# Attention results re-laid with 128-column one-hot products, eight per unit instead of sixteen

## The chip, the cores and the metric

The kernel runs on one core of a Trainium2 chip. The metric is the device time of one execution in microseconds (us), as the median of several runs. Inputs and outputs are in the chip's main memory; the kernel loads them by DMA, computes on five engines that run side by side (PE for matrix products, DVE, ACT and POOL for elementwise work, SP for issuing transfers) and writes the result back.

## The reference

One decode step of a transformer layer: attention over a sliding window of a cache and a dense layer with the mish activation, both on the normalized input, added to the input.

```python
def reference(A_x, A_k_cache, A_v_cache, A_wq, A_wo, B_x, B_w1, B_b1, B_w2):
    # B=2, Sq=1, D=448; 16 query heads, 8 key heads, Dh=256, window W=4096 of 32768
    def _A_ref(x, k_cache, v_cache, wq, wo):
        q = (x @ wq).reshape(B, Sq, Hq, Dh).transpose(0, 2, 1, 3)
        k = jnp.repeat(k_cache[:, :, Sk - W:, :], rep, axis=1)
        v = jnp.repeat(v_cache[:, :, Sk - W:, :], rep, axis=1)
        p = _softmax(jnp.einsum("bhqd,bhkd->bhqk", q, k) * (Dh ** -0.5), axis=-1)
        o = jnp.einsum("bhqk,bhkd->bhqd", p, v)
        return o.transpose(0, 2, 1, 3).reshape(B, Sq, Hq * Dh) @ wo

    def _B_ref(x, w1, b1, w2):
        h = jnp.einsum("bsd,df->bsf", x, w1) + b1
        sp = jnp.log1p(jnp.exp(-jnp.abs(h))) + jnp.where(h > 0, h, 0)
        return jnp.einsum("bsf,fd->bsd", h * jnp.tanh(sp), w2)

    xn = _layernorm(A_x, axis=-1)
    return A_x + _A_ref(xn, A_k_cache, A_v_cache, A_wq, A_wo) + _B_ref(xn, B_w1, B_b1, B_w2)
```

Everything is bf16. The window of keys and values, 2 x 8 x 4096 x 256 numbers each, is by far the largest part of what is read.

## The kernel before

**Units.** The 8 key heads are taken in U = 4 units. A unit holds KU = 2 key heads for both batch rows, J = 4 pairs in all, and as rep = 2 query heads share a key head, NQ = 8 rows of scores. For each unit two k tiles of 4 MB (`load_k`, L97) and four v tiles of 2 MB (`load_v`, L105) are read, and the unit's rows of wo (`load_wo`, L112 and, for the last unit, L118). All of these are issued on SP's queue in the order of the program text; a load waits there until its buffer is free: two buffers for k, three for v (shared at the start with wq and w1), two for wo.

**Work of a unit.** DVE transposes the k tiles (`turns`, L269). PE computes scores (L336 for the mask, L347), ACT takes the exponential (L355), DVE transposes the result into the probabilities p (L358). `weigh` (L370, L378) sums them for the denominator. `values` (L392) multiplies p with the v tiles into PSUM, `gather` (L406 on ACT, L412 on PE) collects this into 8 columns per half, and `finish` (L439, DVE) divides by the denominator. What results is the tile `oT`: 128 partitions by (c, head, batch), where element m of partition p and c is result 2p + c of the head.

**Re-laying.** For units 0, 1 and 2, wo is read with 8 consecutive rows per partition, so that a partition of wo covers one key head and one query head and 8 neighbouring results. `relay` (L455, L464) brings oT into that order with one-hot matrices `hot` (set up on POOL at L147 and L149): for each of the two query heads h of a key head, four y and two k, a product of a 64-column one-hot matrix with the 4 columns of that head fills 64 rows of the PSUM tile `ox_ps`. ACT copies the whole to `ox` in bf16, and `mix_early` (L474) multiplies the 8 slices of ox with wo and adds to the accumulator `early`. The last unit has no relay: its wo is read in another order and `mix` uses oT directly (L249).

**Order.** The order of instructions on each engine is that of the program text. Relays of units 0 and 1 stand after `weigh(u + 1)`; PE goes on to the next unit's values after the mix. The relay of unit 2 stands in the last unit, after `values(3, 0)`; then come its mix, `carry` (L236, L238: the sum so far moves into the accumulator `acc`) and `values(3, 1)`.

**Start and end.** At the start the constants are set up on POOL and DVE, x is normalized, and `project` makes q from wq: its result is copied by ACT to `q_sb` (L300), transposed and spread into `qd`. The dense layer's first half runs early (L504 and on); its second half, `dense_out`, comes last. It multiplies the activation with w2, which arrives in four parts (L547) of 784, 448, 224 and 112 KB after the last v tile; 14 slices with four products each (L249), the last part holding one slice. Then DVE and ACT copy the four quarters of acc to `res` (L620, L622), and SP writes it out (L623).

Of the kernel before, what the change touches and what calls it, by code (L numbers as in the profile page):

```python
# [11 lines left out]
BF16 = mybir.dt.bfloat16  # L12
FP32 = mybir.dt.float32
# [4 lines left out]
def kernel(  # L18
# [13 lines left out]
    nc = tc.nc  # L32
    P = 128
# [5 lines left out]
    Bsz, Sq, D = A_x.shape  # L39
# [3 lines left out]
    rep = Hq // Hkv  # L43
# [3 lines left out]
    KU = J // Bsz  # L47
# [27 lines left out]
    consts = ctx.enter_context(tc.tile_pool(name="consts", bufs=1))  # L75
    small = ctx.enter_context(tc.tile_pool(name="small", bufs=2))
# [6 lines left out]
    ps_m = ctx.enter_context(tc.tile_pool(name="ps_m", bufs=1, space=PSUM))  # L83
# [54 lines left out]
    ident = consts.tile([P, P], BF16)  # L138
# [4 lines left out]
    nc.gpsimd.memset(ones[:], 1.0)  # L143
    id2 = consts.tile([Bsz, Bsz], FP32)
    nc.vector.tensor_copy(out=id2[:], in_=ident[0:Bsz, 0:Bsz])
    hot = consts.tile([P, KU, 4, 32, KU], BF16)
    nc.gpsimd.memset(hot[:], 0.0)  # L147
    for k in range(KU):
        nc.gpsimd.tensor_copy(  # L149
            out=hot[:, k, :, :, k], in_=ident[:].rearrange("p (q y) -> p y q", y=4)  # L150
        )
    eps_t = consts.tile([Bsz, 1], FP32)
    nc.vector.memset(eps_t[:], 1e-5)
# [7 lines left out]
        out=rstd[:], in_=mv[:, 1:2], func=ACT.Sqrt, bias=eps_t[:], scale=1.0  # L161
# [4 lines left out]
        out=xn_bf[:],  # L166
# [8 lines left out]
        out=parm[:], in_=ident[:].rearrange("p (a o) -> p o a", o=2), axis=AXIS.X, op=ALU.add  # L175
# [3 lines left out]
        out=jm[:],  # L179
        in_=ident[:].rearrange("p (a j h) -> p j a h", j=J, h=rep),  # L180
# [4 lines left out]
        out=jm[:], in0=jm[:], scalar1=-1.0, scalar2=29952.0, op0=ALU.add, op1=ALU.mult  # L185
# [3 lines left out]
        out=mneg[:], in_=jm[:].unsqueeze(1).to_broadcast([P, TH * 8, J])  # L189
    )  # L190
    sel = consts.tile([P, 2, NQ], FP32)
    for x in range(2):
        for w in range(4):
# [4 lines left out]
            else:  # L198
                nc.vector.tensor_tensor(
                    out=sel[:, x, :], in0=sel[:, x, :], in1=src, op=ALU.add  # L200
# [16 lines left out]
    for odd in range(2):  # L217
        for half in range(2):
            o = (half + odd) % 2
            nc.vector.tensor_scalar(  # L220
                out=xs[:, odd::2, half * Bsz : (half + 1) * Bsz],
# [55 lines left out]
    for n in range(2):  # L277
        for e in range(2):
# [3 lines left out]
                out=sp[:],  # L282
                in_=ident[:, o : o + 63 : 2].unsqueeze(1).to_broadcast([P, G, 32]),
# [3 lines left out]
    def project():  # L287
        q_ps = ps_m.tile([P, 512], FP32, tag="m", name="q_ps")
        for s in range(NS):
            for u in range(U):  # L290
                nc.tensor.matmul(  # L291
                    q_ps[32 * u : 32 * (u + 1), :],
                    lhsT=xs[:, s, :],
                    rhs=wq_t[s][:, u * 512 : (u + 1) * 512],
                    start=(s == 0),
                    stop=(s == NS - 1),
                    skip_group_check=True,
                )
        q_sb = consts.tile([P, 4, P], BF16)
        nc.scalar.copy(out=q_sb[:].rearrange("p a m -> p (a m)"), in_=q_ps[:])  # L300
        qt_ps = ps_m.tile([P, 4, P], BF16, tag="m", name="qt_ps")
        for a in range(4):
            nc.tensor.transpose(qt_ps[:, a, :], q_sb[:, a, :], ident[:])
        qT = consts.tile([P, 2, U, Bsz, KU, rep], BF16)
        q_v = qt_ps[:].rearrange("p (h c) (u r) -> p c u r h", c=2, u=U)
        for c in range(2):
            for b in range(Bsz):
                nc.vector.tensor_copy(
                    out=qT[:, c, :, b, :, :], in_=q_v[:, c, :, b : KU * Bsz : Bsz, :]
                )  # L310
        qr_ps = ps_m.tile([P, 2 * NB, U, NQ], FP32, tag="m", name="qr_ps")
        for n in range(NB):
            for e in range(2):
                nc.tensor.matmul(
                    qr_ps[:, 2 * n + e, :, :].rearrange("p u q -> p (u q)"),
                    lhsT=spread[n % 2, e][:].rearrange("p g a -> p (g a)"),
                    rhs=qT[:, n // 2].rearrange("p u b k h -> p (u b k h)"),
                    start=True,
                    stop=True,
                    skip_group_check=True,  # L320
                )
        for g in range(G):
            rows = slice(g * 32, (g + 1) * 32)
            nc.vector.tensor_copy(
                out=qd[rows, :, :, g, :],
                in_=qr_ps[rows].rearrange("p n u q -> p u n q"),
            )
# [119 lines left out]

    def relay(u):
        oT = state.pop(("oT", u))
        ox_ps = ps_m.tile([P, 4, 2, Bsz], FP32, tag="m", name="ox_ps")  # L450
        for h in range(rep):
            rows = slice(h * 64, (h + 1) * 64)
            for y in range(4):
                for k in range(KU):
                    nc.tensor.matmul(  # L455
                        ox_ps[rows, y, :, :],
                        lhsT=hot[:, k, y, :, :].rearrange("p q k -> p (q k)"),
                        rhs=oT[:, :, k * rep + h, :],
                        start=(y == 0 and k == 0),
                        stop=(y == 3 and k == KU - 1),  # L460
                        skip_group_check=True,
                    )
        ox = small.tile([P, 8, Bsz], BF16, tag="ox", name="ox")
        nc.scalar.copy(  # L464
            out=ox[:].rearrange("p i b -> p (i b)"),
            in_=ox_ps[:].rearrange("p y c b -> p (y c b)"),
        )
        state["ox", u] = ox

    def mix_early(u):  # L470
# [89 lines left out]
    load_w1()  # L560
    turns(0, 0)
    project()
    scores(0, 0)
    turns(0, 1)
# [4 lines left out]
    for u in range(U - 1):  # L569
        load_k(u + 1, 0)  # L570
        load_v(u, 0)
        load_v(u, 1)
        load_k(u + 1, 1)
        load_v(u, 2)
        load_v(u, 3)
        load_wo(u)
        turns(u + 1, 0)
        values(u, 0)
        values(u, 1)
        scores(u + 1, 0)  # L580
        turns(u + 1, 1)
        values(u, 2)
        values(u, 3)
        gather(u)
        finish(u)
        scores(u + 1, 1)
        weigh(u + 1)
        if u < U - 2:
            relay(u)
            mix_early(u)  # L590
# [9 lines left out]
    for g in range(G - 1):  # L600
        values(u, g)
        if g == 0:
            relay(u - 1)
            mix_early(u - 1)
            carry()
# [48 lines left out]
```

The softmax here doesn't subtract the row's maximum and nothing guards it: scores larger than these inputs give would overflow.

## Time and profile before

| | |
|---|---|
| median of 6 runs | 190.72 us (190.63 to 191.07) |
| the profiled execution | 190.64 us |
| its span, first to last instruction | 188.4 us |
| PE busy | 86.1 us, 873 products and 873 weight loads |
| DVE busy | 89.4 us |
| ACT busy | 12.3 us |
| POOL busy | 4.0 us |
| granted PE clock, mean | 0.775 |
| read from main memory | 77.67 MB, 412 GB/s over the span |

The profile shows one execution. A line of its timeline gives start and length in us, the engine, the line of the program, the operation, what it writes and reads, the shape, how many were merged, and in brackets how long the engine was idle before and what ended that. PEld is PE's weight load, which overlaps its products; SPq and ACTq are the issuing of transfers. The chain of waits is followed back from the last instruction: at each step to what released it. "issue" in it is time in which an engine waited for nothing that the profile shows. In the strip of digits a digit is the busy share, in tenths, of one fortieth of the span.

The part of the page on single groups has, for the line of the relay, 48 loads of 64 columns at a median of 113 ns and 48 products at 171 ns, starting between 86.0 and 169.3 us, in three bursts of 16; and three copies on ACT at 172 ns.

### The profile page before, as it was taken

How to read it: one execution, taken by the hardware profiler on the slowest of the kernel's cores; microseconds unless marked ns; L12 is line 12 of the kernel's file. 1: busy time of each engine (PE TensorE's matmuls, PEld its weight loads, DVE VectorE, ACT ScalarE, POOL GpSimd, SP SyncE). 2: the span in 40 equal slices, each digit the busy share in tenths (PEclk: the TensorE clock that was granted, in tenths of full speed). 3: DMA queues.
4: the chain of work that ended last, by engine and by line, in shares of the span. 5: the costliest groups of instructions: out<-in, count | busy, mean ns of one | idle time of the engine just before them, and what ended most of it. 6: DMA issues, size and time to landing. Idle time of an engine off the chain costs nothing.

```text
span 188.4 us, 1989 instructions
## 1 busy us (share of the span) xinstructions
PE 86.1 (46%) x873; PEld 36.7 (20%) x873; DVE 89.4 (47%) x81; ACT 12.3 (7%) x23; POOL 4.0 (2%) x16
## 2 busy tenths in 40 slices
PE   0301545565139004878345033867272044966493
PEld 0100121521012001423011011422021011522192
DVE  6619643983990098018930395039900692040001
ACT  3000031001000000110001000110001001011101
POOL 8000000000000000000000000000000000000000
PEclk9999999999999955566858855586759755599655
DMA  6999999998999999999999999999998999999990
GB/s 223 445 390 412 444 424 425 472 442 386 435 459 410 414 443 410 463 438 403 428 480 424 403 424 455 415 435 417 452 459 386 438 414 445 428 407 439 412 382 26
DMA packets 5871, 77.78 MB, mean 413 GB/s; under 512 B 868, under 2 KB 1640, under 8 KB 2408
## 3 DMA queue, kind: packets, MB, share of 16 engines
q1 hardware_dynamic: 5588, 77.66, 96.7%
q8 instruction: 6, 0.10, 0.2%
q10 hardware_dynamic: 276, 0.01, 0.1%
q14 instruction: 1, 0.01, 0.0%
HBM read 77.67 MB, written 0.00 MB: 412 GB/s over the span
## 4 chain that ended last, share of the span: by engine, by line
DMA 83%; PE 8%; issue 3%; DVE 3%; SPq 1%; ACT 0%; DVEq 0%; ACTq 0%
DMA v<-in_A_v_cache_dram 68%; DMA k<-in_A_k_cache_dram 15%; PE pv L392 5%; DVE kt L269 2%; PE acc L249 1%; PE o L412 1%; PE o L427 1%; SPq L134 1%; SPq L97 1%; ACT vs L406 0%; DVEq L649 0%; DVE res L620 0%; DVE h_sb L518 0%; DVE oT L439 0%; ACTq L406 0%
## 5 line engine op out<-in xcount | busy, mean ns | idle before, releaser
L269 DVE STREAM_TRANSPOSE kt<-k 128x4096 f32<-128x4096 f32 x16 | 70.1, 4421 | 40.5 <-DMA k<-in_A_k_cache_dram 40.5
L392 PE MATMUL pv<-v,p 128*32 128x512 bf16 x240 | 25.1, 560 | 61.2 <-DMA v<-in_A_v_cache_dram 61.2
L347 PE MATMUL sc<-kt,qd 128*32 128x512 bf16 x256 | 24.1, 539 | 3.3 <-DVE kt L269 1.9
L392 PEld LDWEIGHTS <-p 128*32 128x32 bf16 x240 | 8.1, 120 | 76.5 <-issue 69.0
L439 DVE TENSOR_TENSOR oT<-o,rec 128x16 bf16<-128x16 f32 x4 | 0.7, 174 | 30.0 <-PE o L412 16.3
L358 DVE STREAM_TRANSPOSE p<-ex 128x512 bf16<-128x512 bf16 x8 | 5.2, 690 | 15.1 <-ACT ex L355 15.1
L347 PEld LDWEIGHTS <-qd 128*32 128x32 bf16 x256 | 7.9, 124 | 17.9 <-issue 14.6
L355 ACT ACTIVATE ex<-sc 128x512 bf16<-128x512 f32 x8 | 4.8, 597 | 72.5 <-PE sc L347 72.5
L291 PE MATMUL q_ps<-wq,xs 128*32 128x512 bf16 x28 | 3.4, 625 | 11.8 <-DMA wq<-in_A_wq_dram 11.8
L412 PE MATMUL o<-sel,vs 128*128 128x8 f32 x32 | 7.5, 364 | 2.8 <-ACT vs L406 2.8
L412 PEld LDWEIGHTS o<-sel,vs 128*128 128x128 f32 x32 | 7.1, 326 | 6.4 <-ACT vs L406 6.4
L474 PE MATMUL early<-wo,ox 128*2 128x448 bf16 x24 | 8.0, 498 | 0.8 <-ACT ox L464 0.8
L370 PE MATMUL dn<-p,ones 128*128 128x512 bf16 x8 | 3.5, 433 | 6.4 <-DVE p L358 6.4
L406 ACT COPY vs<-pv 128x512 f32<-128x512 f32 x4 | 2.3, 586 | 54.3 <-PE pv L392 54.3
L336 PE MATMUL sc<-mneg,ident 128*128 128x512 bf16 x8 | 4.8, 595 | 0.0
L504 PE MATMUL h_ps<-xs,w 128*128 128x4 bf16 x49 | 2.8, 193 | 4.2 <-DMA w<-in_B_w_dram 4.2
L212 PE MATMUL xr_ps<-ident,xrows 2*128 2x2 bf16 x7 | 1.0, 181 | 6.7 <-DVE xrows L211 6.7
L378 DVE TENSOR_REDUCE rec<-dn 128x8 f32<-128x512 f32 x4 | 2.8, 692 | 2.1 <-PE dn L370 2.1
L504 PEld LDWEIGHTS <-w 128*128 128x128 bf16 x49 | 2.7, 154 | 5.1 <-DMA w<-in_B_w_dram 5.1
L291 PEld LDWEIGHTS <-xs 128*32 128x32 bf16 x28 | 1.0, 126 | 13.8 <-issue 13.8
L474 PEld LDWEIGHTS <-ox 128*2 128x2 bf16 x24 | 2.3, 104 | 4.6 <-issue 3.0
L370 PEld LDWEIGHTS <-ones 128*128 128x128 bf16 x8 | 0.5, 99 | 8.5 <-DVE p L358 6.2
(62 smaller groups left out, 38.1 us busy)
## 6 DMA issues: line engine op xcount, KB each, us to landing
k<-in_A_k_cache_dram SPq DMA_DIRECT2D x8, 4096.0 KB, 30.0
v<-in_A_v_cache_dram SPq DMA_DIRECT2D x15, 2048.0 KB, 27.1
wo<-in_A_wo_dram SPq DMA_DIRECT2D x3, 896.0 KB, 24.7
wq<-in_A_wq_dram SPq DMA_DIRECT2D x1, 2048.0 KB, 16.7
w<-in_B_w_dram SPq DMA_DIRECT2D x1, 1568.0 KB, 31.9
wq<-in_A_wq_dram SPq DMA_DIRECT2D x1, 1536.0 KB, 19.7
v<-in_A_v_cache_dram SPq DMA_DIRECT2D x1, 1536.0 KB, 11.0
wo<-in_A_wo_dram SPq DMA_DIRECT2D x2, 448.0 KB, 15.3
```

The source lines that it names most:

```text
L269: nc.vector.transpose(out=kt[i][:, :, :, r, :], in_=t[:, r * KE : (r + 1) * KE].bitcast(FP32).rearrange("p (a c j) -> p a c j", c=P // (R ...
L291: nc.tensor.matmul(q_ps[32 * u : 32 * (u + 1), :], lhsT=xs[:, s, :], rhs=wq_t[s][:, u * 512 : (u + 1) * 512], start=(s == 0), stop=(s == N ...
L336: nc.tensor.matmul(sc[:].rearrange("p t c m -> p (t c m)"), lhsT=ident[:], rhs=mneg[:].rearrange("p a j -> p (a j)"), start=True, stop=Fal ...
L347: nc.tensor.matmul(sc[32 * w : 32 * (w + 1)].rearrange("p t c m -> p t (c m)"), lhsT=qd[:, u, 2 * n + e, :, :].rearrange("p g q -> p (g q) ...
L355: nc.scalar.activation(out=ex[:, :, :, i, :], in_=sc[:], func=ACT.Exp, scale=scale)
L358: nc.vector.transpose(out=p_t[h][:].rearrange("p g t q -> p t g q"), in_=ex[:, h * TH : (h + 1) * TH].rearrange("p t c i m -> p t (c i m)" ...
L370: nc.tensor.matmul(dn[:].rearrange("p a q -> p (a q)"), lhsT=ones[:], rhs=p_t[i][:].rearrange("p g t q -> p (g t q)"), start=(i == 0), sto ...
L378: nc.vector.tensor_reduce(out=rec[:], in_=dn[:].rearrange("p a q -> p q a"), axis=AXIS.X, op=ALU.add)
L392: nc.tensor.matmul(pv[32 * w : 32 * (w + 1), :, :].rearrange("p x d -> p (x d)"), lhsT=p_t[a // 4][:, g, 4 * (a % 4) : 4 * (a % 4) + 4, :] ...
L412: nc.tensor.matmul(po[:, c, :], lhsT=sb[:, x, c::2], rhs=sel[:, x, :], start=(x == 0 and c == 0), stop=(last and x == 1), skip_group_check ...
L474: nc.tensor.matmul(early[:], lhsT=ox[:, i, :], rhs=w[:, i, :], start=False, stop=(u == U - 2 and i == 7),)
L504: nc.tensor.matmul(h_ps[:, i, :, :].rearrange("p k b -> p (k b)"), lhsT=w1_v[:, s, i, :], rhs=xs[:, s, 0 : 2 * Bsz], start=(s == 0), stop= ...
```

## The change

The one-hot matrices get a second copy side by side, so that one matrix has 128 columns: 64 for each of the two query heads. One product then takes the columns of both heads of a key head (8 instead of 4) and fills all 128 rows of `ox_ps`, which has twice the columns. Of its rows, the upper half is wanted for one head and the lower half for the other; two copies on ACT, of 64 partitions each, pick these out where one copy of 128 partitions took all. There are 8 products per unit instead of 16. `hot` doubles to 2 KB per partition; `q_sb` of 1 KB per partition moves from its own place into the buffer `vs`, which the gathers use later.

```diff
-    hot = consts.tile([P, KU, 4, 32, KU], BF16)
+    hot = consts.tile([P, KU, 4, rep, 32, KU], BF16)
     nc.gpsimd.memset(hot[:], 0.0)
     for k in range(KU):
         nc.gpsimd.tensor_copy(
-            out=hot[:, k, :, :, k], in_=ident[:].rearrange("p (q y) -> p y q", y=4)
+            out=hot[:, k, :, :, :, k],
+            in_=ident[:].rearrange("p (q y) -> p y q", y=4).unsqueeze(2)
+            .to_broadcast([P, 4, rep, 32]),
         )
...
-        q_sb = consts.tile([P, 4, P], BF16)
+        q_sb = small.tile([P, 4, P], BF16, tag="vs", name="q_sb", bufs=1)
...
     def relay(u):
         oT = state.pop(("oT", u))
-        ox_ps = ps_m.tile([P, 4, 2, Bsz], FP32, tag="m", name="ox_ps")
+        ox_ps = ps_m.tile([P, 4, 2, rep, Bsz], FP32, tag="m", name="ox_ps")
+        for y in range(4):
+            for k in range(KU):
+                nc.tensor.matmul(
+                    ox_ps[:, y, :, :, :].rearrange("p c h b -> p (c h b)"),
+                    lhsT=hot[:, k, y, :, :, :].rearrange("p h q k -> p (h q k)"),
+                    rhs=oT[:, :, k * rep : (k + 1) * rep, :].rearrange("p c h b -> p c (h b)"),
+                    start=(y == 0 and k == 0),
+                    stop=(y == 3 and k == KU - 1),
+                    skip_group_check=True,
+                )
+        ox = small.tile([P, 8, Bsz], BF16, tag="ox", name="ox")
         for h in range(rep):
             rows = slice(h * 64, (h + 1) * 64)
-            for y in range(4):
-                for k in range(KU):
-                    nc.tensor.matmul(
-                        ox_ps[rows, y, :, :],
-                        lhsT=hot[:, k, y, :, :].rearrange("p q k -> p (q k)"),
-                        rhs=oT[:, :, k * rep + h, :],
-                        start=(y == 0 and k == 0),
-                        stop=(y == 3 and k == KU - 1),
-                        skip_group_check=True,
-                    )
-        ox = small.tile([P, 8, Bsz], BF16, tag="ox", name="ox")
-        nc.scalar.copy(
-            out=ox[:].rearrange("p i b -> p (i b)"),
-            in_=ox_ps[:].rearrange("p y c b -> p (y c b)"),
-        )
+            nc.scalar.copy(
+                out=ox[rows].rearrange("p (y c) b -> p y c b", c=2), in_=ox_ps[rows, :, :, h, :]
+            )
         state["ox", u] = ox
```

## The prediction

> **What bounds the kernel.** I read the DMA part of the page first, then the chain of waits, the timeline around each relay, and the end.
>
> ```profile
> DMA  6999999998999999999999999999998999999990
> q1 hardware_dynamic: 5588, 77.66, 96.7%
> q8 instruction: 6, 0.10, 0.2%
> ...
> DMA 83%; PE 8%; issue 3%; DVE 3%; SPq 1%; ACT 0%; DVEq 0%; ACTq 0%
> ```
>
> The transfers fill the 16 engines from the second slice to the last but one: 77.66 MB take the time they take, and most of the chain is DMA. Work on PE, ACT or POOL counts only where it moves the start or the end, or lets the queue run dry. The queue stays full around every relay: the mean share is 0.89 from 86.0 to 86.6, 0.82 from 126.9 to 127.6 and 1.23 from 168.8 to 169.7.
>
> The timeline of PE around the first relay, and from the last relay on (start, length, instruction, idle time before it):
>
> ```profile
> 86.02 0.57 PE L455 MATMUL ox_ps<-oT,hot 128*64 128x4 bf16 x16
> 86.85 3.14 PE L474 MATMUL early<-wo,ox 128*2 128x448 bf16 x8 [0.26 <-ACT ox L464]
> 92.19 0.40 PE L392 MATMUL pv<-v,p 128*32 128x512 bf16 x4 [2.20 <-DMA v<-in_A_v_cache_dram]
> ...
> 168.88 0.57 PE L455 MATMUL ox_ps<-oT,hot 128*64 128x4 bf16 x16
> 169.71 1.67 PE L474 MATMUL early<-wo,ox 128*2 128x448 bf16 x8 [0.26 <-ACT ox L464]
> ...
> 176.42 0.62 PE L392 MATMUL pv<-v,p 128*32 128x512 bf16 x4 [3.02 <-DMA v<-in_A_v_cache_dram]
> ```
>
> Each relay and its mix are followed by idle time that ends with a landing: 2.20 us in unit 0, 2.17 in unit 1 (PE waits until 133.11), 3.02 after the last. So the relay has a cover in all three places.
>
> The end, from the chain of waits, and the last transfer (KB, us from issue to landing):
>
> ```profile
> 182.90 2.19 PE acc L249 x59
> 185.09 0.28 issue
> 185.37 0.45 PE acc L249 x11
> 185.82 0.24 DVE res L620
> ...
> w<-in_B_w_dram SPq DMA_DIRECT2D x1, 112.0 KB, 13.3
> ```
>
> This last w2 part was issued at 171.81 and lands at 185.10. PE should go on some 0.04 us later: it started the part before at 184.84, after a landing at 184.80. It doesn't. The first of that part's 8 products starts at 184.84, the second only at 185.373, 0.53 us later, though it waits for no semaphore; the profile writes "issue". The 4 products of the last part, whose data were there at 185.10, go behind the hole, so **the hole and not the last landing sets the end**.
>
> **What the hole is.** I take it for PE waiting for its own code. Queue q8 fetches code six times, 16 KB each, starting at 39.7, 62.7, 96.4, 130.0, 163.6 and 182.98. In order of time PE has started 267, 465, 695, 989, 1238 and 1594 of its instructions (loads and products both) by then, a mean of 265 apart. The sixth takes until 183.86, and the hole follows 1.5 us later, at instruction 1729 of 1754. Elsewhere PE needs 20 us and more between two fetches; only in the last stretch does it run through 265 of them (1464 to 1729) in under 4 us, from 180.9 on. No other break of this length without a wait shows in the order of PE's starts.
>
> The Trainium skill ("Runtime: NRT & Kernel Launch", Instruction fetch mechanics) says that code comes in 16 KiB blocks of 256 instructions, the next one fetched while the current one runs, and that crossing a boundary is mostly hidden. The packet size agrees; by "mostly hidden" the change would be worth 0, by the row the boundary costs 0.53 us here.
>
> **The change, part by part.**
>
> *Relay on PE.* 16 loads of 64 columns and 16 products become 8 and 8 of 128 columns, in three units: 24 loads and 24 products go. L455 takes 0.57 us for 16. For 8 with 128 columns there are two rows. L314, eight of 128*128, takes 0.38 (25.22 to 25.60). L504, 49 of 128*128 by 4 columns, starts one every 54 ns: 8 x 0.054 + 0.14 = 0.57. I take 0.38, since L314 too is a burst of 8; so -0.19, between -0.19 and 0 a unit. A rule speaks against it: the skill ("TensorE: Matmul & The Clock Gate", Step-by-step: what each phase is for) has load time grow with the column count, by which half as many loads of twice the width save nothing. The rows don't show that: the 64-column load of L455 has 113 ns, the 128-column load of L314 104 ns.
>
> *Two copies on ACT for one.* L464 has 172 ns for 128x16; two of 64x16 at the same price with 30 ns between cost +0.20 (bounds 0, if half the rows cost half and follow at once, and +0.25). The mix on PE waits for the second; nothing else stands behind it on ACT before the next exponential some 15 us later, or, in the last unit, the copy of L236, itself late with the mix.
>
> *Sum of a relay:* -0.19 + 0.20 = about 0, bounds -0.2 to +0.25, hidden by the 2.2, 2.17 and 3.02 us above; without that cover at most 3 x 0.25 = 0.75. In unit 2, SP's issue of the last v tile at 168.99 is put down to the relay by the profile, but that tile's buffer is read by the products of L392 just ahead of the relay; were it the relay, the issue would move by 0.2 us in front of a full queue. The change issues no transfer and passes no queue.
>
> *Setup on POOL.* The memset of 128x512 (0.52) becomes 128x1024; that of qd has this shape and 0.95: +0.43. The two copies of 0.33 double: +0.65. Together +1.08 (bounds +0.43 and +1.7). Behind them on POOL stand the memset of xs (ends 3.62, needed by DVE at 7.76) and the spread copies (end 4.61, needed at 25.19). DVE may be slowed meanwhile: its 2x2 cast at 1.33 lasts 1.48 us and ends with the hot memset. But DVE idles 4.88 us before the first k tile at 13.25, PE 10.18 before wq. Price 0; if that cover were gone, up to 1.7 us.
>
> *q_sb moves* into the buffer that the gathers use: written at 23.37, read until 24.62, next written at 77.50. Its 1 KB per partition is what hot gains. Price 0; with the cover gone the copy would wait for four transposes of 0.6 us.
>
> *48 fewer PE instructions.* PE then has 1706 where the hole comes at 1729: it would fall behind the last product. The last 4 products start at 185.10 + 0.04 = 185.14. From a product's start to its reader's there are now 0.33 us (ACT: 185.512 to 185.847; DVE: 185.432 to 185.805, less 0.044 behind its predecessor). So DVE's first result copy starts at 185.47 instead of 185.805: **-0.34 us**, and all that follows moves along. Bounds: 0, if the hole is not code or moves to another place before the end; -0.53, if the whole hole goes and the landing comes earlier too.
>
> **Sum.** The profiled execution took 190.64 us: a span of 188.4 and 2.2 around it. 190.64 - 0.34 = 190.30. The median of the runs is 0.08 above the profiled one: 190.72 - 0.34 = **190.38**, which is -0.18%. What tells apart from no change here is about 0.2%, 0.38 us, just above my term.
>
> **The rivals.**
>
> *A, forecast (0.64):* as above, 190.2 to 190.6. For it: a break without a wait, in the one place where PE consumes code fastest. 0.25 of this chance lies beyond 0.2%, 0.39 within.
>
> *B, nothing happens (0.15):* the hole is no matter of code, or boundaries move with something else, and the relays are hidden. 190.72. For it: one execution shows the hole, once. Against: nothing else explains products standing that wait for nothing.
>
> *C, more than the hole (0.08):* 0.53 us or somewhat more, 190.15, if the last landing also comes earlier. It is late by five of the sixteen engines: these report the last part between 184.86 and 185.10, ten others between 183.38 and 183.66. One more engine is late after each of the first five code fetches. With fewer of them late the end would come earlier; but one late engine is enough, and no fetch before the last goes.
>
> *D, slower, by the sixth fetch (0.13 with the setup and unknowns):* 48 instructions at 4 us / 265 = 15 ns each start it 0.72 us later, near 183.7. Each earlier fetch left an engine 1.49 us late (means 185.01 and 183.52). If the sixth meets an engine that is late already, before its last row ends at 184.80, the landing goes to 186.59, DVE starts at 186.59 + 0.04 + 0.33 = 186.96 instead of 185.805, and the time is 190.72 + 1.15 = 191.9. It decides from any start before 184.8 on one of these five. Against: the five fetches each took an engine that was on time, and the sixth began at 182.98, when an on-time engine had just ended.
>
> **How the numbers follow.** Faster by over 0.2%: 0.25 + 0.08 = 0.33. Within: 0.39 + 0.15 = 0.54. Slower: 0.13. The range, 190.1 to 190.95, leaves out the far end of D and little of C, and takes in the runs of B, most of which lie between 190.63 and 190.85.
>
> **What would show it.** Right: PE x849; L455 x24 with N = 8, about 0.38 us a burst; POOL near 5 us; the last 12 products of L249 without a break of 0.5 us, the last four right behind a landing near 185.1; six fetches still; idle time before the mixes within 0.2 us of now. Wrong: the same hole again near the end (B), a last landing near 186.6 (D), or PE coming to L392 after its landing in any unit, for then the relays were not covered.

## The result

The changed kernel takes 190.18 us (median of 18 runs, 189.77 to 190.49) against 190.77 for the kernel before in the same series (36 runs, 190.46 to 191.23): a ratio of 0.9965, with a 95% interval of 0.9958 to 0.9972. That is faster by about 0.35%, 0.67 us by the ratio and 0.59 by the medians. The prediction was 190.38, or 0.18% less.

The profiled execution of the changed kernel took 190.37 us with a span of 188.2. From its page, the DMA part and the engines of the chain:

```profile
DMA  6989999998999999999999999999999999999990
q1 hardware_dynamic: 5588, 77.66, 96.8%
q8 instruction: 6, 0.10, 0.2%
...
DMA 83%; PE 8%; issue 3%; DVE 3%; SPq 1%; ACT 0%; DVEq 0%; ACTq 0%
```

Nothing has moved here: the same bytes fill the same time, and there are six code fetches still. PE's timeline around the first and from the last relay (lines of the program behind the relay are numbered 1 or 2 higher than before):

```profile
86.12 0.34 PE L455 MATMUL ox_ps<-oT,hot 128*128 128x8 bf16 x8
86.91 2.65 PE L475 MATMUL early<-wo,ox 128*2 128x448 bf16 x8 [0.44 <-ACT ox L466]
92.12 0.62 PE L394 MATMUL pv<-v,p 128*32 128x512 bf16 x4 [2.57 <-DMA v<-in_A_v_cache_dram]
...
169.08 0.35 PE L455 MATMUL ox_ps<-oT,hot 128*128 128x8 bf16 x8
169.87 1.67 PE L475 MATMUL early<-wo,ox 128*2 128x448 bf16 x8 [0.44 <-ACT ox L466]
...
176.54 0.62 PE L394 MATMUL pv<-v,p 128*32 128x512 bf16 x4 [2.98 <-DMA v<-in_A_v_cache_dram]
```

A burst of products takes 0.34 us instead of 0.57, the wait for ACT 0.44 instead of 0.26. From the first product of a relay to the first of its mix there were 0.83 us and are 0.79. PE still waits 2.5 to 3 us for the next v tile, so this 0.04 us is hidden three times. The end, from the chain of waits, and the last part of w2 (KB, us from issue to landing):

```profile
183.02 2.54 PE acc L251 x60
185.56 0.25 DVE res L621
...
w<-in_B_w_dram SPq DMA_DIRECT2D x1, 112.0 KB, 13.2
```

The "issue" of 0.28 us between two groups of the accumulator's products is gone. The last part lands at 185.22, 0.12 later than in the profile before; its first product starts at 185.263, 0.04 later, and the copies of the result begin at 185.55 instead of 185.805. The end now follows the last landing.

### The profile page after: what moved, and what is told of

Same layout as the page of the kernel before. It is cut to its first block, busy times and chain, and to the rows that moved or that the text cites. A ratio compares the mean times of both kernels' runs of the same rounds, so it can differ in the third digit from the quotient of the medians.

```text
span 188.2 us, 1944 instructions
## 1 busy us (share of the span) xinstructions
PE 87.2 (46%) x849; PEld 36.7 (20%) x849; DVE 89.8 (48%) x81; ACT 12.8 (7%) x26; POOL 4.7 (2%) x16
## 4 chain that ended last, share of the span: by engine, by line
DMA 83%; PE 8%; issue 3%; DVE 3%; SPq 1%; ACT 0%; DVEq 0%; ACTq 0%
DMA v<-in_A_v_cache_dram 68%; DMA k<-in_A_k_cache_dram 15%; PE pv L394 5%; DVE kt L271 2%; PE acc L251 1%; PE o L414 1%; PE o L429 1%; SPq L134 1%; SPq L97 1%; ACT vs L408 0%; DVEq L650 0%; DVE res L621 0%; DVE h_sb L519 0%; DVE oT L441 0%; ACTq L408 0%
## 5 line engine op out<-in xcount | busy, mean ns | idle before, releaser
L394 PE MATMUL pv<-v,p 128*32 128x512 bf16 x240 | 26.8, 593 | 59.3 <-DMA v<-in_A_v_cache_dram 59.3
L349 PE MATMUL sc<-kt,qd 128*32 128x512 bf16 x256 | 25.8, 572 | 3.2 <-DVE kt L271 1.8
L475 PE MATMUL early<-wo,ox 128*2 128x448 bf16 x24 | 7.0, 451 | 1.3 <-ACT ox L466 1.3
L145 DVE CAST id<-ident 2x2 f32<-2x2 bf16 x1 | 1.9, 1911 | 1.3 <-POOL ident masks.py:199 1.3
```

What stands on the lines that cost most here:

```text
L349: nc.tensor.matmul(sc[32 * w : 32 * (w + 1)].rearrange("p t c m -> p t (c m)"), lhsT=qd[:, u, 2 * n + e, :, :].rearrange("p g q -> p (g q) ...
L394: nc.tensor.matmul(pv[32 * w : 32 * (w + 1), :, :].rearrange("p x d -> p (x d)"), lhsT=p_t[a // 4][:, g, 4 * (a % 4) : 4 * (a % 4) + 4, :] ...
L475: nc.tensor.matmul(early[:], lhsT=ox[:, i, :], rhs=w[:, i, :], start=False, stop=(u == U - 2 and i == 7),)
```

## The experiments

Each ratio is to runs of the kernel before on the same chip, in two groups: its median is 190.86 us beside the first four kernels and 190.74 beside the other four. A "pair" is a weight load and a product of two columns, put ahead of the projection, where PE waits for wq (lines of the program behind it are numbered 10 higher):

```diff
+    pad_ps = ps_m.tile([P, 2], FP32, tag="m", name="pad_ps")
+    for _ in range(24):
+        nc.tensor.matmul(
+            pad_ps[0:32, :],
+            lhsT=ident[:, 0:32],
+            rhs=ident[:, 0:2],
+            start=True,
+            stop=True,
+            skip_group_check=True,
+        )
     early = ps_e.tile([Bsz, D], FP32)
```

**The kernel before, again.** No edit.

> The kernel before, unchanged, to see its spans in many executions beside its times. Theory A (PE waits at the end for the code block that begins at its instruction 1729): time 190.7 to 190.8, spans near 188.4, the hole of about 0.5 us in the last 12 products of dense_out again. Rival R1 (the gain is of the relay or the setup, and the hole a matter of one execution): the same time, but no hole, or one at another place.

Measured: 190.80 us (11 runs), ratio 0.9999 (0.9990 to 1.0008). The timeline of the end in its profile:

```profile
184.07 1.20 PE L249 MATMUL acc<-w,act_bf 128*2 128x112 bf16 x33
...
185.60 0.44 PE L249 MATMUL acc<-w,act_bf 128*2 128x112 bf16 x11 [0.33 <-issue]
...
186.03 0.56 DVE L620 CAST res<-acc 2x112 bf16<-2x112 f32 x2 [3.00 <-PE acc L249]
```

Again 11 products stand behind a hole, in another execution: the hole belongs to the program. But it ends at 185.60, not 185.37, and most spans are longer than in the profile that I predicted from: 188.3 to 189.0, mean 188.66 in 29 executions of the kernel before, where that profile has 188.4.

**The changed kernel with 24 pairs.** PE has as many instructions as before; the relay is that of the change.

> The changed kernel with 24 more pairs of weight load and 2-column product on PE, early (between 8 and 18 us, where PE is idle); they write a tile that nobody reads. PE has then as many instructions as before. Theory A: the hole comes back at the same place, in the second product of w2's third part, and the time goes back to about 190.6 to 190.8. Rival R1: stays at 190.2, no hole. Rival R2 (the gain is fewer instructions on PE as such): half or all of it lost, without a hole.

Measured: 190.62 us (11 runs), ratio 0.9994 (0.9985 to 1.0002): the gain is gone. The end:

```profile
184.82 0.08 PEld L261 LDWEIGHTS <-act_bf 128*2 128x2 bf16 x1 [0.18 <-issue]
185.68 0.45 PE L261 MATMUL acc<-w,act_bf 128*2 128x112 bf16 x11 [0.60 <-issue]
```

The hole is back at the same product, the second of w2's third part, 0.85 us from start to start, 0.60 of it idle.

**The changed kernel with 64 pairs.** As above with 64.

> The changed kernel with 64 more such pairs. Theory A: the block boundary falls 128 instructions earlier in the program's text, among the products of values_fixed, and its block is asked for before 177 us, over 4 us before PE needs it: no hole, 190.1 to 190.3, although PE has 80 instructions more than before. Rival R1: 190.2 too. Rival R2: slower than with 24 pairs, 190.9 or more.

Measured: 190.16 us (5 runs), ratio 0.9961 (0.9948 to 0.9974). More instructions than with 24 pairs, and faster: a rule of so much time for an instruction (R2) is out. PE has no break at the end but four waits for parts of w2, each over 0.04 us after a landing.

**The kernel before with 104 pairs.** The decisive one: no line of the change in it.

> The kernel before, its 16 products of 64 columns, one copy and small one-hot tile untouched, with 104 more such pairs: 208 instructions, which with the 48 that the change takes away make 256, so that code blocks lie at the end as in the changed kernel. Theory A: no hole, and 190.2 to 190.4, the time of the changed kernel or nearly; seven code fetches instead of six. Rival R1: 190.8 as before. Rival R2: 191 or more.

Measured: 190.13 us (12 runs), ratio 0.9969 (0.9959 to 0.9979), the gain of the changed kernel without the changed relay. The end:

```profile
184.08 1.52 PE L259 MATMUL acc<-w,act_bf 128*2 128x112 bf16 x44
...
185.63 0.56 DVE L630 CAST res<-acc 2x112 bf16<-2x112 f32 x2 [2.59 <-PE acc L259]
```

The products run without a break, and the copies start at 185.63 where they start at 186.03 in the kernel before of the same group. Its page counts seven code fetches, "q8 instruction: 7, 0.11, 0.2%". R1 is out: relay, copies and setup are worth nothing that shows beside this, 190.13 against 190.18.

The next three move the boundary on, to see how the hole comes and goes.

**The changed kernel with 12 pairs.**

> The changed kernel with 12 early pairs of load and product that nobody reads. Theory A: the block boundary falls just behind the last product of dense_out (about 1702 of the changed kernel's PE instructions are done by then, the boundary is at 1729 less 24): no hole, 190.1 to 190.3, where 24 pairs took 190.62. Rival R2 (number of PE instructions as such): half way between, 190.4.

Measured: 189.99 us (5 runs), ratio 0.9961 (0.9948 to 0.9973). No hole; the whole gain, not half.

**The changed kernel with 36 pairs.**

> The changed kernel with 36 such pairs: the boundary falls in the second part of w2, about 22 products before the end, and its block is asked for near 180.9 us. Theory Q (the fetch waits behind all rows that its DMA engine still has, so it starts at 183.0 to 183.4 whenever it is asked for, and PE goes on 2.37 us after its start, as in the three executions with a hole): PE goes on at about 185.6 with 22 products left, 0.5 us; the time is 191.0 to 191.2, slower than before. Theory L (the fetch starts a fixed 1.4 to 1.9 us after it is asked for): it starts at 182.3 to 182.8, PE goes on by 185.2, and the time is 190.2 to 190.7.

Measured: 190.45 us (11 runs), ratio 0.9991 (0.9976 to 1.0006). In the packets of the trace the sixth fetch starts at 182.48, earlier than in any other kernel with a hole, so theory L holds here and Q does not. PE does stop once, as the loads show:

```profile
184.52 0.09 PEld L261 LDWEIGHTS <-act_bf 128*2 128x2 bf16 x5 [0.24 <-issue]
184.83 0.59 PEld L261 LDWEIGHTS <-act_bf 128*2 128x2 bf16 x22 [0.21 <-issue]
```

It stops until 184.83 with 23 products left, where 24 pairs left 11: the break has moved by the 12 pairs that were added. But the data of the last parts are not there yet, so nothing is lost: the copies begin at 185.63, and the spans have a mean of 188.23, within 0.13 of the changed kernel's 188.10. That the median is above 190.2 all the same lies outside the span: there it takes 2.34 us in the mean (2.03 to 3.18) instead of the changed kernel's 2.04. This kernel has a seventh fetch, at 185.98, while the program is ending; that it causes this was not tried.

**The changed kernel with 48 pairs.**

> The changed kernel with 48 such pairs: the boundary falls near the start of w2's second part, some 34 products before the end, and its block is asked for by 177.4 us at the latest. Theory Q (waits behind all rows that its engine still has): start at 183.0 to 183.4 again, PE goes on at 185.6 with 0.8 us of products left, 191.3 to 191.5. Theory L, or a wait of up to 5.2 us as the sixth fetch of the kernel with 64 pairs had (asked for by 172.2, started at 177.4): start by 182.6, a hole of at most 0.9 us or none, 190.1 to 190.8.

Measured: 190.16 us (6 runs), ratio 0.9971 (0.9959 to 0.9983). The sixth fetch starts at 180.17 and there is no hole. Q would have it at 183 and the kernel 0.6 us slower than before; it is out. The fixed delay of L is out as well, if the block is asked for where the expectation puts it: 180.17 is 2.8 us after 177.4, not 1.4 to 1.9. What sets the start of a fetch stays open.

**The setup alone.** The kernel before with the changed constants and place of q_sb:

```diff
-    hot = consts.tile([P, KU, 4, 32, KU], BF16)
+    hot = consts.tile([P, KU, 4, rep, 32, KU], BF16)
...
-        q_sb = consts.tile([P, 4, P], BF16)
+        q_sb = small.tile([P, 4, P], BF16, tag="vs", name="q_sb", bufs=1)
...
-                        lhsT=hot[:, k, y, :, :].rearrange("p q k -> p (q k)"),
+                        lhsT=hot[:, k, y, 0, :, :].rearrange("p q k -> p (q k)"),
```

> The kernel before with the setup of the changed one alone: the one-hot tile doubled and filled on POOL, q_sb in the gathers' buffer; the relay keeps its 16 products of 64 columns and its one copy. Theory A: the time of before, 190.7 to 190.9, with the hole in the last products; POOL near 4.7 us. Rival R3 (the setup moves the start and with it the end): 190.2 to 190.5, or over 191.

Measured: 190.89 us (11 runs), ratio 1.0004 (0.9995 to 1.0013). The time of before, and the hole of before, ahead of the same 11 products:

```profile
185.82 0.45 PE L251 MATMUL acc<-w,act_bf 128*2 128x112 bf16 x11 [0.60 <-issue]
```

R3 is out.

Put together, in the executions that were profiled (the fetch's start from the trace's packets, PE from the order of its starts; the time is the median of the kernel's runs):

| kernel | sixth fetch starts | PE goes on | after | last landing | time |
|---|---|---|---|---|---|
| before, first profile | 182.98 | 185.37 | 2.40 | 185.10 | 190.72 |
| before, again | 183.26 | 185.60 | 2.34 | 185.28 | 190.80 |
| changed, 24 pairs | 183.30 | 185.68 | 2.37 | 185.08 | 190.62 |
| setup alone | 183.49 | 185.82 | 2.34 | 185.22 | 190.89 |
| changed, 36 pairs | 182.48 | 184.83 | 2.35 | 185.30 | 190.45 |
| changed | 183.32 | no hole | | 185.22 | 190.18 |
| changed, 12 pairs | 183.36 | no hole | | 185.19 | 189.99 |
| changed, 48 pairs | 180.17 | no hole | | 185.28 | 190.16 |
| changed, 64 pairs | 177.40 | no hole | | 185.44 | 190.16 |
| before, 104 pairs | (seventh) 183.21 | no hole | | 185.30 | 190.13 |

PE goes on 2.34 to 2.40 us after the fetch starts, whenever that is, in five executions. That, and the boundary that moves with the count of instructions, shows that PE waits for its code. PE's clock is no rival: from 182.9 to 186.0 the granted clock is 0.50 in all ten profiles.

## Why the prediction was right, and where its size was off

**What bounds the kernel**: right. DMA share and bytes are the same, the last landing is within 0.2 us, and the end is set by what follows the last landing, or by the hole.

**The relay on PE**: -0.19 us predicted, -0.23 measured (0.57 to 0.34), just outside the bound of -0.19, since the products of 128 columns start some 25 ns apart, those of 64 some 27 in the mean, and the load is even shorter:

```profile
L455 PEld LDWEIGHTS <-hot x24: 95/96/98, 85.9 to 169.2; 128*128 128x128 bf16 x24
L455 PE MATMUL ox_ps<-oT,hot x24: 166/166/179, 86.1 to 169.3; 128*128 128x8 bf16 x24
```

The columns are the least, median and greatest length in ns, then first and last start. The load has a median of 96 ns with 128 columns and had 113 with 64. The Trainium skill's rule that load time grows with the columns ("TensorE: Matmul & The Clock Gate", Step-by-step: what each phase is for) does not show in these two rows. Nor does a load of 128 columns have one length: the prediction weighed L314's 104 ns against the rule and left out L504, where the same shape takes 154 ns in the median, at a granted clock of 1.00 in both places.

**Two copies on ACT**: +0.20 predicted; 0.35 us together for 0.17 before, +0.18. The sum of a relay, "about 0", is -0.04 us, and it is hidden.

**Setup on POOL**: +1.08 predicted, +0.7 measured (busy 4.0 to 4.7). The memset is as predicted, the copies were taken too high:

```profile
2.27 0.95 POOL L147 MEMSET hot<- 128x1024 bf16 x1
3.29 0.85 POOL L149 COPY hot<-ident 128x256 bf16<-128x256 bf16 x2
4.05 0.28 POOL L218 MEMSET xs<- 128x224 bf16 x1
```

Twice the elements cost 0.47 us a copy instead of 0.33, not 0.65. DVE's last step of the setup moves from 7.76 to 8.25 and it still idles 4.58 us before the first k tile. The setup alone has a ratio of 1.0004: hidden, as said.

**The hole and the 48 instructions**: the mechanism is right and shown, by putting the instructions back (24 pairs), by shifting the boundary without the change (104 pairs), and by the boundary's other places. (The prediction's count of 1754 holds 8 semaphore and drain instructions beside the 873 loads and 873 products, and its "1.5 us later" runs to the hole's end; neither changes the argument.) The **size** of this term was off: -0.34 us predicted for the end. The mean span fell from 188.66 (29 executions; 188.63 in the 22 of the other group) to 188.10, -0.56 us. The step that failed is in the working of this term: it takes the hole's end, 185.373, and the landing, 185.10, from one execution, and carries that landing and the 0.33 us over to the changed kernel. In that execution the fetch started early, at 182.98; the three others with a lasting hole have 183.26 to 183.49.

With my own working (landing + 0.04 + 0.33 against the start of DVE's first copy) the four give -0.34, -0.38 (185.65 for 186.03), -0.66 (185.45 for 186.11) and -0.66 (185.59 for 186.25), a mean of -0.51. But the two of -0.66 are from executions some 0.15 to 0.18 us longer than the mean of their kernels, 24 pairs and setup alone. The second profile of the kernel before, whose span of 188.65 is the mean one, gives only -0.38, because its landing was late too. From it to the profile of the changed kernel the copies moved by 0.48 (186.03 to 185.55): 0.38 by the working, 0.06 because the landing is at 185.22 instead of 185.28, and 0.04 because the first copy follows the first of the last four products by 0.29 us and not by 0.33. The profiled execution of the changed kernel is itself 0.06 longer than the mean of 188.10. So the term was short by several small pieces, and the early profile is only one of them; that the landing is earlier as a rule is not shown (185.08 to 185.30 in the profiles with a lasting hole or the covered one, 185.19 to 185.44 in those without).

The median of the runs stood only 0.08 us above the profiled one and did not tell of this, as its span of 188.4 was near the least of 188.3 to 189.0.

The other 0.1 us or so lies outside the span: 2.15 us in the mean before (29 executions), 2.04 after (18); spans are on record to 0.1 us, so a single value is good to 0.05. Six of the changed kernel's 18 executions have 1.75 to 1.84 us there, and eight of the 22 of the kernels with 64, 104 and 12 pairs have 1.69 to 1.82; none of 84 executions with the lasting hole (the kernel before in both groups and again, 24 pairs, setup alone) went below 2.0. Yet none of the six with 48 pairs, which have no hole either, did so (2.04 to 2.24), and 36 pairs have more, not less. So the missing hole alone does not explain it, and what shortens it was not found.

**The rivals.** B, nothing happens, fails with the hole gone. C, more than the hole, is nearest in size (190.15 for 190.18), but not by its mechanism: the last landing is no earlier (185.22 against 185.10 and 185.28), and five engines are still late. D, the sixth fetch on a late engine, did not come about: in the changed kernel it starts at 183.32, and the last landing is in its place. I had put it at 183.7; it moved by at most 0.34 us.

**Where the number fell.** 190.18 lies inside the range of 190.1 to 190.95, but just below the 190.2 to 190.6 of the forecast A, and the gain is nearly twice the 0.18% predicted. That it stayed in the range was partly luck: the 0.1 us from outside the span was in no term.

## What to carry to other kernels

Where an engine runs through its last instructions in a burst behind a full DMA queue, look for breaks that wait for no semaphore, and count its instructions: a few dozen more or fewer, anywhere earlier, move such a break out of the end or into it. A gain or loss of some tenths of a per cent from an edit that is hidden by every view may be that, and a pad of idle instructions tells it apart. And where the end is a race of two things, size it from several executions, not from the one that was profiled.

## What the runs showed of the hardware

Code fetches cost in two ways. PE went on 2.34 to 2.40 us after a fetch of 16 KB started, in five executions. That is hidden where 23 us and more pass from one fetch to the next, as among the first five of the kernel before; no break shows at the five crossings that belong to them. It was not hidden in the last stretch, where PE runs through as many instructions in under 4 us: there the boundary cost 0.53 to 0.86 us from one product to the next. The Trainium skill ("Runtime: NRT & Kernel Launch", Instruction fetch mechanics) calls the crossing of such a boundary mostly hidden, which agrees with the first five and not with the last.

And behind each fetch in the full stream one DMA engine reports some 1.5 us after the others, to the end of the kernel: in the kernel before, ten engines report the last part of w2 between 183.38 and 183.66 and five between 184.86 and 185.10, and one more becomes late after each of the first five fetches. With 104 pairs six fetches have gone before, and six engines are late, from 184.92 to 185.30. Since one late engine is enough, the seventh fetch cost nothing that shows: the last landing there was 185.30, against 185.10 and 185.28 in the two profiles of the kernel before.
